# Decay rows of one head pair issued from ScalarE's queue in an attention and mixer kernel

## The chip, the cores and the metric

The kernel runs on one core of a Trainium2 chip. The metric is the device time of one execution in microseconds (us), lower is better. Of the core's engines, TensorE (PE) multiplies matrices, VectorE (DVE) and ScalarE (ACT) work element by element, GpSimd (POOL) does masks and issues most of the loads, and SyncE (SP) issues transfers. Each engine takes its instructions strictly in the order in which they stand in its own queue. A transfer (DMA) is issued by an instruction on one of these queues and tells that it has landed by a semaphore.

## The reference, cut to what matters

Eight batches of eight heads go through causal attention with a decay from a running sum, and the result goes through a mixer. The part that the change touches is the decay bias:

```python
s_pos = np.maximum(s, 0.0)
cum = np.cumsum(s_pos, axis=-1)
bias = -(cum[:, :, :, None] - cum[:, :, None, :])
scores = np.where(causal, -1000000000.0, scores + np.minimum(bias, 0.0))
```

Then follow the softmax, the product with `v`, the low-rank mixing over the sequence (`x + (xT @ U @ V)T`) and a two-layer channel mix with a residual (512 to 2048 to 512).

## The kernel before, in words

Heads are worked on in pairs: pair `n` is heads `2n` and `2n+1`, and batch 0 is the pairs 0 to 3. Each of these pairs has a buffer, a slot: partitions 0 to 63 hold the transposed `q` and `k` of both heads, and partitions 64 to 67 hold four decay rows. With them one matrix product over 68 partitions gives scores and decay bias together. The decay rows are not computed in a slot: DVE and ACT compute them for all 64 heads at once into a tile `rows` (it lies in the buffer that the profile calls `hT`; lines 221 to 228), and small transfers of 9 KB, four rows of 2304 bytes for one head, bring them to the slots (line 231). There are eight of these for batch 0, all on SP's queue, two for each pair, in the order of the pairs. After them SP stores the rows of the later batches in memory (`rows_hbm`, line 238), from where later slots are filled (line 299).

The start of the kernel, up to some 35 us, is written out by hand as a list of `step` calls (lines 1011 to 1082). The queues of DVE, ACT and SP are fixed to the order in which the program issues (`in_program_order`, line 1083). So the place of a call in the list is the place of its instructions on every engine. The pieces of the list that matter here are:

- `T0` to `T3`: the transposes of a pair on PE (line 315) into PSUM banks, and their copies into the slot (line 338). `copies` (line 289) decides who copies: of pairs 0 and 1 ACT copies the first head and DVE the second; of pair 2 ACT copies the first of four pieces and DVE the other three; of pair 3 DVE copies all four.
- `A` and `B_`: most of the scores of pair 0, which do not wait for the slot's decay rows but take them from `rows` (`near_by_rows`, line 364). Each ends with an exponential on ACT (line 395).
- `S0` to `S3`: the scores from the slots (line 402), with exponentials on ACT (lines 417, 428 and 434). A weight load of line 402 waits for the decay rows of its head.
- `spin`: products on a constant tile, whose result is not used (line 216).

PSUM has two pools here: four banks `pwork`, taken in turn, and two double banks `pscore`, taken in turn. A piece that takes a bank waits until the work on what it held before is done. POOL applies the causal masks for these four pairs (line 150), and issues loads in between.

Completion semaphores for the transfers of SP and ACT are eight counters, which the framework gives out in turn. A transfer that gets a counter for the second time waits at its issue until the counter's earlier transfer has landed. In the kernel before, the eighth row transfer waits in this way for the load of `s`, and the two stores to `rows_hbm` for the two row transfers of pair 0.

From about 35 us on, a list of words and loops interleaves the attention of later batches with the mixer of earlier ones, up to the end.

Of the kernel before, what the change touches and what calls it, by code (L numbers as in the profile page):

```python
# [39 lines left out]
def kernel(  # L40
# [12 lines left out]
    nc = tc.nc  # L53
# [11 lines left out]
    PB = NP // B  # L65
# [160 lines left out]
    nc.vector.tensor_sub(rest, cum, rows[:, 0, 1, :])  # L226
    nc.vector.tensor_copy(rows[:, 1, 1, :], rest)
    nc.vector.tensor_sub(rows[:, 2, 1, :], rest, rows[:, 1, 1, :])
    for n in range(PB):
        for hh in range(2):  # L230
            nc.sync.dma_start(
                out=slots[n][D:KA, hh, 0 : 2 * S],
                in_=rows[2 * n + hh : 2 * n + hh + 1].rearrange("n r c s -> n r (c s)"),
            )

    rows_hbm = nc.dram_tensor("rows_hbm", (4, BH, S), BF16, kind="Internal").ap()
    for r, n_r, c in ((0, 3, 1), (3, 1, 0)):
# [766 lines left out]
    def step(*gens):  # L1004
        for gen in gens:
            next(gen, None)

    def spin_some(n, ps=None):
        spin(n, (ps or pscore)()[:, 0:512])
# [7 lines left out]
    step(T0)  # L1017
    spin_some(2)
    step(T0, T0)
    step(A, A, A, A)  # L1020
    step(T1, T1, T1)
    step(B_)
# [210 lines left out]
```

The softmax here doesn't subtract the row's maximum and nothing guards it: scores larger than these inputs give would overflow.

## Time and profile before

| | |
|---|---|
| median of 13 runs | 364.79 us |
| lowest and highest of these | 364.05 and 366.83 us |
| the profiled execution's own time | 364.79 us |
| its span in the profile | 363.1 us |
| PE busy | 353.4 us (97% of the span) |
| DVE busy | 278.4 us (77%) |
| ACT busy | 209.5 us (58%) |
| POOL busy | 84.6 us (23%) |
| data moved | 37.41 MB, mean 103 GB/s |

A row of the timeline gives the start, the time from start to end of a group of like instructions, the engine (SPq is SP's queue), the source line, the operation, what it writes and reads, how often, and in brackets for how long the engine sat idle before it and what ended the wait. Instructions of one engine overlap a little in these rows: an exponential that is listed with 1.02 us is followed by the next after about 0.92 us.

### The profile page before, as it was taken

The page shows a single profiled execution, that of the slowest core. Times are in us where ns is not written, and L with a number is a line of the kernel's source. Part 1 is how long each engine was busy: PE and PEld are TensorE (multiplying, and loading weights), DVE is VectorE, ACT ScalarE, POOL GpSimd, SP SyncE. Part 2 cuts the span into 40 slices and gives each one's busy share as a digit, 9 for nine tenths or more (in the row PEclk, how much of TensorE's full clock was granted, in tenths as well). Part 3 has the DMA queues.
Part 4 walks back from the last instruction along what each step waited for, and adds up shares of the span by engine and source line. Part 5 has one row for each costly group of instructions (what it writes and reads, how often), then busy time and mean ns, then how long its engine had stood idle before and what let it go on. Part 6 is the DMA issues. An engine that isn't in the chain of part 4 may idle for free. (4 is left out here: it accounts for less than half of the span.)

```text
span 363.1 us, 9627 instructions
## 1 busy us (share of the span) xinstructions
PE 353.4 (97%) x4031; PEld 255.2 (70%) x4031; DVE 278.4 (77%) x607; ACT 209.5 (58%) x319; POOL 84.6 (23%) x108
## 2 busy tenths in 40 slices
PE   8999999999999999999999999999999999999995
PEld 3675566666588667876689667876688568678884
DVE  8875776779789758985699559975899279676976
ACT  3874975747762678247843686357834641565710
POOL 8997444314040403040314012000000000000000
PEclk9999999999999999999999999999999999999999
DMA  7999999999989998989994999271013401500063
GB/s 106 172 197 204 168 178 107 157 140 139 115 51 107 130 141 59 97 99 118 127 107 62 143 135 86 50 151 37 18 49 91 94 18 32 147 0 31 29 117 116
DMA packets 153027, 37.41 MB, mean 103 GB/s; under 512 B 136600, under 2 KB 151352, under 8 KB 152984
## 3 DMA queue, kind: packets, MB, share of 16 engines
q0 software_dynamic: 110016, 18.50, 82.9%
q1 hardware_dynamic: 42680, 18.11, 29.1%
q8 instruction: 31, 0.51, 0.6%
q10 hardware_dynamic: 288, 0.20, 0.2%
q14 instruction: 12, 0.10, 0.1%
HBM read 37.25 MB, written 9.70 MB: 129 GB/s over the span
## 5 line engine op out<-in xcount | busy, mean ns | idle before, releaser
L648 PE MATMUL pwork<-uT,w_sb 128*128 128x512 bf16 x464 | 116.6, 379 | 0.7 <-ACT hT L929 0.5
L417 ACT ACTIVATE pT<-pscore 128x1024 bf16<-128x1024 f32 x56 | 57.2, 1030 | 55.1 <-PE pscore L402 54.1
L929 ACT ACTIVATE hT<-pwork 128x512 bf16<-128x512 f32 x108 | 65.2, 609 | 31.2 <-PE pwork L648 31.1
L648 PEld LDWEIGHTS <-w_sb 128*128 128x128 bf16 x480 | 41.2, 98 | 37.3 <-issue 0.7
L402 PE MATMUL pscore<-slot 68*128 68x320 bf16 (+1 forms) x500 | 56.0, 246 | 0.2
L402 PEld LDWEIGHTS <-slot 68*128 68x128 bf16 x564 | 41.2, 97 | 16.8 <-issue 1.3
L693 PEld LDWEIGHTS <-hT 128*128 128x128 bf16 x496 | 46.1, 98 | 7.2 <-issue 0.7
L186 POOL DMA_DIRECT2D v_slot<-in_v_dram x36 | 30.3, 854 | 81.6 <-PE pwork L462 71.1
L693 PE MATMUL pwork<-w_sb,hT 128*128 128x256 bf16 x384 | 48.2, 273 | 0.0
L347 DVE TENSOR_TENSOR pT<-pT,keep 128x512 bf16<-128x512 bf16 (+1 forms) x81 | 28.7, 354 | 21.0 <-ACT pT L417 14.8
L335 DVE COPY slot<-pwork 64x576 bf16<-64x576 bf16 x76 | 34.4, 453 | 4.7 <-PE pwork L315 3.9
L462 PEld LDWEIGHTS <-pT 128*128 128x128 bf16 x870 | 32.4, 98 | 5.3 <-issue 0.6
L462 PE MATMUL pwork<-v_slot,pT 128*128 128x65 bf16 x870 | 35.5, 194 | 0.2 <-DVE uT L516 0.2
L693 PE MATMUL pwork<-w_sum,slot 128*128 128x256 bf16 x256 | 32.0, 273 | 0.8 <-DVE o_sb L707 0.7
L472 DVE TENSOR_TENSOR x_sb<-pwork,rec 128x320 bf16<-128x320 f32 x64 | 31.2, 489 | 1.3
L428 ACT ACTIVATE pT<-pscore 128x1024 bf16<-128x1024 f32 x29 | 30.2, 1042 | 2.6 <-PE pscore L402 2.4
L471 DVE RECIPROCAL rec<-pwork 128x5 f32<-128x5 f32 x64 | 12.2, 191 | 20.7 <-PE pwork L462 20.3
L693 PEld LDWEIGHTS <-slot 128*128 128x128 bf16 x256 | 24.0, 98 | 4.6 <-issue 1.6
L338 DVE COPY slot<-pwork 64x576 bf16<-64x576 bf16 x29 | 23.2, 801 | 5.1 <-PE pwork L315 3.3
L112 POOL DMA_DIRECT2D q_sd<-in_q_dram x6 | 12.6, 2105 | 44.9 <-PE pwork L315 41.3
L707 DVE TENSOR_TENSOR o_sb<-o_sb,pwork 128x512 f32<-128x512 f32 (+2 forms) x34 | 22.0, 651 | 0.7 <-PE pwork L693 0.3
L315 PEld LDWEIGHTS <-q_sd 72*128 72x128 bf16 x256 | 14.9, 97 | 8.7 <-DMA q_sd<-in_q_dram 0.9
(161 smaller groups left out, 502.1 us busy)
## 6 DMA issues: line engine op xcount, KB each, us to landing
out_dram<-o_sb SPq DMA_DIRECT2D x35, 256.0 KB
w_sb<-in_moe_w_ch_dram POOLq DMA_DIRECT2D x4, 1024.0 KB, 12.4
v_slot<-in_v_dram POOLq DMA_DIRECT2D x28, 128.0 KB, 7.1
q_sd<-in_q_dram POOLq DMA_DIRECT2D x5, 576.0 KB, 13.8
k_sd<-in_k_dram POOLq DMA_DIRECT2D x5, 576.0 KB, 17.1
q_sd<-in_q_dram POOLq DMA_DIRECT2D x4, 288.0 KB, 12.4
k_sd<-in_k_dram POOLq DMA_DIRECT2D x4, 288.0 KB, 11.4
q_sd<-in_q_dram POOLq DMA_DIRECT2D x4, 144.0 KB, 4.7
```

The costliest lines, as they stand in the source:

```text
L186: nc.gpsimd.dma_start(out=vt[:rows_t, t, :, 0:D], in_=v[b, :, ds(t * 128, rows_t), :].rearrange("h p d -> p h d"),)
L335: copies(n, hh, par)(by_run[:, :, :, par, :], src)
L338: copies(n, hh, par)(in_turn[:, :, :, :, par], src.rearrange("p c t m -> p c m t"))
L347: nc.vector.tensor_tensor(dst, dst, keep[:, :, 0:w].to_broadcast([128, n_tiles, w]), op=ALU.min)
L402: nc.tensor.matmul(dst, lhsT=slot[0:KA, hh, ds(S + j * 128, 128)], rhs=slot[0:KA, hh, lo:hi], start=True, stop=True,)
L417: nc.scalar.activation(pT[:, hh, 0:1024], near, EXP, scale=scale)
L428: nc.scalar.activation(pT[:, :, 1024:1536], mid.rearrange("p (a b) -> p a b", a=2), EXP, scale=scale)
L462: nc.tensor.matmul(po[:, i, :], lhsT=pT[:, hh, ds(place(j, i), 128)], rhs=vt[:, j, h, :], start=(j == 0), stop=(j == i), skip_group_check= ...
L472: nc.vector.tensor_tensor(x_sb[:, hp, :, ds(hh * D, D)], po[:, :, 0:D], rec.to_broadcast([128, 5, D]), op=ALU.mult,)
L648: nc.tensor.matmul(f1, lhsT=w1_sb[:, kt, ds(nf * 128, 128)], rhs=u[:, kt, :], start=(kt == 0), stop=(kt == 3),)
L693: nc.tensor.matmul(acc[:, i, :], lhsT=a[:, kt, ds(i * 128, 128)], rhs=b[:, kt, :], start=(i == 0 and kt == 0), stop=(kt == HF - 1), skip_g ...
L929: nc.scalar.activation(hT[:, nf, :], f1, RELU)
```

## The change

The row transfers of pairs 0, 2 and 3 stay on SP's queue, in that order. The two of pair 1 are issued from ACT's queue, behind the third step of `T0` and ahead of `A`.

```diff
-    for n in range(PB):
+
+    def rows_to_slot(n, queue):
         for hh in range(2):
-            nc.sync.dma_start(
+            queue.dma_start(
                 out=slots[n][D:KA, hh, 0 : 2 * S],
                 in_=rows[2 * n + hh : 2 * n + hh + 1].rearrange("n r c s -> n r (c s)"),
             )
+
+    for n in (0, 2, 3):
+        rows_to_slot(n, nc.sync)
...
     step(T0)
     spin_some(2)
     step(T0, T0)
+    rows_to_slot(1, nc.scalar)
     step(A, A, A, A)
     step(T1, T1, T1)
     step(B_)
```

The built program then has these waits on ACT's queue (line 232 is the transfer, 342 the copy that was line 338, 399 the exponential that was line 395):

```
L342 copy slot0 x2            waits for PE
L232 transfer slot1, head 0   waits for DVE and ACT (the rows are computed)
L232 transfer slot1, head 1   waits for completion counter 1
L399 exponential of A         waits for PE
L342 copy slot1 x2            waits for PE
L342 copy slot2               waits for PE
L399 exponential of B_        waits for PE
```

Completion counter 1 belongs to the first row transfer of pair 0, on SP's queue. Compute instructions stand in the same order as before on every engine.

## The prediction

> **What bounds the kernel now.** I read the page first, for the engine that is never idle, then the waits, for how long it is, and then the timeline of the first 20 us, engine by engine, since the change lies there.
>
> ```profile
> PE 353.4 (97%) x4031; PEld 255.2 (70%) x4031; DVE 278.4 (77%) x607; ACT 209.5 (58%) x319; POOL 84.6 (23%) x108
> PE   8999999999999999999999999999999999999995
> ACT  3874975747762678247843686357834641565710
> PEclk9999999999999999999999999999999999999999
> DMA  7999999999989998989994999271013401500063
> ```
>
> The reader is to see that PE is full from the second slice of nine us to the last but one, while ACT is not. There is no slack behind the opening in which lost time could be won back: in the waits of PE after 24 us the longest sum is 0.9 us, and none of them is for a transfer. So what the opening loses should be lost at the end. In the opening itself PE is not alone in the bound. This is ACT's part of the timeline:
>
> ```profile
> 6.45 1.61 ACT L338 COPY slot<-pwork 64x576 bf16<-64x576 bf16 x2 [0.47 <-PE pwork L315]
> 9.26 1.02 ACT L395 ACTIVATE pT<-pscore 128x1024 bf16<-128x1024 f32 x1 [1.20 <-PE pscore L364]
> 10.18 1.60 ACT L338 COPY slot<-pwork 64x576 bf16<-64x576 bf16 x2
> 12.03 0.80 ACT L338 COPY slot<-pwork 64x576 bf16<-64x576 bf16 x1 [0.25 <-PE pwork L315]
> 13.16 1.02 ACT L395 ACTIVATE pT<-pscore 128x1024 bf16<-128x1024 f32 x1 [0.33 <-PE pscore L364]
> 14.08 1.02 ACT L428 ACTIVATE pT<-pscore 128x1024 bf16<-128x1024 f32 x1
> ```
>
> Between 8.06 us and 9.26 us ACT has nothing to do, and from there to 15 us it has gaps of 0.25 and 0.33 us alone. The hole of 1.20 us is where the change puts two transfers. Now who waits for ACT (DVE), and what PE does (PE):
>
> ```profile
> 12.86 5.76 DVE L338 COPY slot<-pwork 64x576 bf16<-64x576 bf16 x7 [1.34 <-ACT slot L338]
> ...
> 15.38 0.59 PE L216 MATMUL pwork<-busy 128*128 128x512 bf16 x2 [0.26 <-DVE slot L338]
> 15.81 0.61 PE L402 MATMUL pscore<-slot 68*128 68x128 bf16 x6
> 16.25 0.81 PE L216 MATMUL pwork<-busy 128*128 128x512 bf16 x3
> ```
>
> This is a chain: ACT's copy of pair 2 (12.03 to 12.83) lets DVE begin at 12.86 with its three copies for pair 2, and the third ends at about 15.3 (12.86 + 3 x 0.82), when a PSUM bank comes free for PE's spin at 15.38, behind which the scores of pair 1 stand at 15.81. The transfers in question, on SP:
>
> ```profile
> 8.20 5.10 SPq L231 DMA_DIRECT2D slot<-hT  x8
> 13.34 0.92 SPq L238 DMA_DIRECT2D rows_hbm<-hT  x2
> ```
>
> Eight issues, the first of 0.76 us and the later ones 0.57, one each 0.615 us. The landing records in the trace say when all increments of each had come: pair 0 at 12.1 and 12.3 us, pair 1 at 13.8 and 15.76, pair 2 at 16.0 and 16.4. Pair 1's second one is what a weight load of line 402 waits for:
>
> ```profile
> PEld L402 <- DMA slot<-hT: 0.3, 1, 0.3
> ```
>
> That wait ends at 15.80, when the spins of 15.38 (two of 0.21 us each) are through as well.
>
> **The change part by part.**
>
> SP loses two issues, 1.23 us. Pairs 2 and 3 and the stores to `rows_hbm` are issued that much sooner. Nobody waits for them before (no row of the waits names them), so this is worth nothing; the cover is that pair 2's rows, at 16.0 us, are first used at 17.5.
>
> ACT gains two issues. The rows are ready at 8.11 us (DVE line 228), ACT is free at 8.06, so the first goes out at 8.15. A row for an issue on ACT stands at the end of the trace (line 785, two in 0.86 us, 0.43 each); SP's same transfer takes 0.57. I take 0.57; both ends, 0.43 and 0.76, are in the range. Were this all, ACT would be back at about 9.3 us, and the exponential of `A` would be late by nothing or 0.1 us.
>
> But the second issue adds a wait. It gets completion counter 1, and waits for the first row transfer of pair 0, which SP issues at 8.20. That landed at 12.1 us before. It is still SP's first, so it should land then again, give or take 0.3 us for the ACT transfer beside it, which brings 9 KB to the same engines. A rule speaks of this time. The row: issue at 8.20, its first packets at 10.60, landed at 12.1, so 2.4 us to the first packet and 3.9 in all, with the DMA row of the page at 9. The Trainium skill, "DMA: Bandwidth & Descriptors", section "Latency and other measured facts", puts the first byte of a transfer from these queues at about 0.6 us. By the rule the landing would be at 8.20 + 0.6 + 1.5 = 10.3 us, by the trace at 12.1. I take the trace, where the same transfer is measured under the same load.
>
> Behind that wait on ACT's in-order queue stand the exponential of `A`, two copies of pair 1, one of pair 2, and the exponential of `B_`. Followed through:
> - second issue 12.15 to 12.72; exponential of `A` at 12.72 in place of 9.26, late by 3.46;
> - copies of pair 1 from 12.72 + 0.92 = 13.64 to 15.2 (PE had the inputs by 10 us);
> - copy of pair 2 at 15.25 in place of 12.03, late by 3.2: the gap of 0.25 ahead of it is eaten;
> - exponential of `B_` at 16.0 in place of 13.16, late by 2.85.
>
> DVE starts its pair 2 copies at 16.08 in place of 12.86. The third ends at 18.55, so PE's spin goes at 18.6 in place of 15.38, late by 3.2. PE meanwhile stops first for the PSUM of `A` (S0 at 13.7 in place of 13.05), then for the bank that ACT's pair 1 copies hold (15.2), then for pair 2's banks (16.9). All of it is done by 18.6. Scores of pair 1, head 1, then come at 19.0.
>
> The rows of pair 1: the first lands at about 12.2 and is used at 17.2. The second is issued at 12.15; transfers issued between 10.3 and 12.7 took 4.2 to 5.5 us to land, so 16.4 to 17.7, ahead of 19.0. So the 0.33 us wait goes and is worth nothing, as the spins end with it. If the landing took 7 us, it would be next late.
>
> From 18.6 on PE, ACT and DVE have the same work in the same order. PE was busy 4.69 of 5 us between 15 and 20 us and 4.90 of the next 5, so at most some 0.4 us is to be made up; I take 0.2. POOL is late by less: its masks start at 15.52 because of its own issues before, and the load issued at 16.93 goes at about 18.4, but its users are late by 3.2. At 28 us PE stood 0.9 us for nothing the profile shows; it could shrink or grow, plus or minus 0.9.
>
> Sum: 0 (SP) + 3.2 (wait and issue, through DVE's chain) - 0.2 = +3.0 us. The profiled execution's own time, 364.79 us (span 363.1 and 1.7 around it), is the median itself. So 364.8 + 3.0 = **367.8 us**.
>
> A second rule weighs on the gaps. The row: the first nine spins took 3.62 us, 0.40 each, and those at 15.38 take 0.21, so this PE starts at half speed, although the PEclk row says 9 throughout. The Trainium skill, "TensorE: Matmul & The Clock Gate", "Part 1: The HAM clock gate", says the half clock returns after one idle window of about 3.4 us. In the changed kernel PE works some 1.9 us of the 5.5 between 13.05 and 18.6, in pieces no more than 1.1 us apart. No window is idle, so by its wording nothing is lost; if a thin window counts as idle, one window at half speed costs up to 3.4 / 2 = 1.7 us. I leave it at 0, and 1.7 goes to a rival.
>
> **The rivals.**
>
> 1. *The wait is short.* The landing comes as the rule has it, at 10.3. Then the second issue ends at 10.9, `A` at 10.9, pair 2's copy at 10.9 + 0.92 + 1.62 = 13.45, late by 1.4. Time: 366.2. For it: the DMA load might fall differently with another queue in use. Against: the measured 3.9 us.
>
> 2. *The clock falls.* The delay of 3.0 and 1.7 more for half-speed products, 369.5. For it: the opening is padded with spins on a constant tile, so it is meant to be kept busy, and the gaps triple. Against: the longest gap is a third of a window.
>
> 3. *Not slower: the wait is no wait, and ACT's hole covers both issues.* The point from which it decides is the landing of counter 1: before about 9.0 us, ACT is at work by 9.5 and the 0.25 and 0.33 us gaps swallow the rest. Then rows of pair 1 land at about 12.3, the 0.33 us wait on them goes, and the best is 364.8 - 0.33 = 364.5. Against: it needs 0.8 us from issue to landing, where the quickest in the trace, the load of `s`, took from 0.82 to 3.43. That the waits on the counter are not as built is the same case. A late landing that PE makes up later belongs here too, in time: 364.5 to 365.3.
>
> **How the numbers follow.** What a measurement of this kernel can tell from no change is about 0.2%, 0.73 us. Forecast 0.70, its own range 366.6 to 368.9 (landing 0.3 either way, issue -0.15 to +0.2, gap of 28 us, made up 0 to 0.4); rival 1 0.12; rival 2 0.10; rival 3 0.08, of which 0.03 faster by over 0.2% and 0.05 within. All else is slower: 0.92. The range takes in the forecast and rival 1 and stops where rival 2 begins to: 366.1 to 369.4.
>
> **What would show it.** In ACT's timeline: the two issues, with some 3.4 us between the start of the first and of the second, and `A`'s exponential at 12.7 us with no wait for PE; the copy of pair 2 at 15.25. In DVE's: the seven copies at 16.1, with an idle time of 4 us or more ahead of them for ACT. In PE's: the spin before pair 1's second head at 18.6, late by 3.2, and every later row late by about 3. Wrong if `A`'s exponential is at about 9.3, if a row transfer of pair 1 is waited for, or if rows after 40 us are late by less than 1.

## The result, and the profile after

| | us |
|---|---|
| before, median of 48 runs | 364.66 |
| changed, median of 11 runs | 371.26 (lowest 368.40) |
| ratio to before, with its 95% interval | 1.0152 (1.0132 to 1.0173) |
| changed, taken again beside the experiments, median of 6 | 371.40; ratio 1.0181 (1.0127 to 1.0234) |

The change makes the kernel slower by some 6.6 us by the medians. The ratio compares means and leaves out executions more than 1.5% above the fastest of their kernel (of the changed one those of 609.67 and 374.35 us), and by it the loss is some 5.5 us. The direction was forecast, the size was not: 367.8 us in a range of 366.1 to 369.4. The execution that was profiled first took 609.67 us, with PE's clock near half from beginning to end, and none of the others came near it; so all rows below are from a second profile of the same kernel, of an execution of 371.8 us (span 370.1).

The clock that counts here is the granted clock, the share of full speed that the profile shows PE to have been given. The page of that second profile has in its clock row what before had not:

```profile
PEclk9759999999999999999999999999999999999999
```

A digit is a slice of 9.25 us: the second and the third, 9 to 28 us, hold a stretch at half speed. The trace's clock records give it exactly: half from 13.82 to 27.48 us, four times 3.41 us. Busy time by stage from the same profile (start and end, length, then busy us and number of instructions of PE, weight loads, DVE, ACT and POOL, then the granted clock, DMA share and GB/s):

```profile
8.00:12.00 4.00, 4.00 (x59) 2.84 (x57) 3.28 (x5) 0.70 (x1) 3.53 (x9) 1.00 1.13 160
12.00:16.00 4.00, 2.39 (x26) 1.65 (x25) 0.00 (x0) 2.02 (x3) 4.00 (x7) 0.73 1.19 161
16.00:20.00 4.00, 3.01 (x27) 2.20 (x27) 2.59 (x4) 3.27 (x6) 1.56 (x4) 0.50 1.29 186
20.00:24.00 4.00, 4.00 (x20) 2.21 (x19) 3.03 (x4) 2.13 (x3) 2.77 (x7) 0.50 1.07 181
24.00:28.00 4.00, 4.00 (x31) 1.81 (x30) 0.00 (x0) 3.02 (x4) 2.74 (x5) 0.57 0.75 121
```

ACT does 0.70 us of work between 8 and 12 us, and PE is thin (busy for part of the time only) from 12 to 20. From 20 us on PE is full again, but of 20 products in 4 us, which is the half clock. Now ACT's timeline, the hole and what is in it:

```profile
7.08 1.62 ACT L342 COPY slot<-pwork 64x576 bf16<-64x576 bf16 x2 [0.98 <-PE pwork L319]
8.25 5.68 ACTq L232 DMA_DIRECT2D slot<-hT  x2
13.97 1.02 ACT L399 ACTIVATE pT<-pscore 128x1024 bf16<-128x1024 f32 x1 [5.27 <-PE pscore L368]
14.89 2.41 ACT L342 COPY slot<-pwork 64x576 bf16<-64x576 bf16 x3
17.17 1.01 ACT L399 ACTIVATE pT<-pscore 128x1024 bf16<-128x1024 f32 x1
```

The two issues span 5.68 us. In the trace the first took 1.16 us (8.25 to 9.41) and the second 0.59 (13.33 to 13.92); between them ACT waited for completion counter 1, whose last increment came at 13.31. The row of 13.97 puts its idle time down to PE; but PE's last products for `A` were done at 9.54 (a row of line 368, 8.94 and 0.60 long), and what released ACT is the landing. In between ACT did none of the work that stands behind the issue in its queue. This is what a wait for a transfer looks like when the engine's next compute row carries it. DVE and PE behind it:

```profile
17.33 5.76 DVE L342 COPY slot<-pwork 64x576 bf16<-64x576 bf16 x7 [5.51 <-ACT slot L342]
```

```profile
15.04 1.01 PE L406 MATMUL pscore<-slot 68*128 68x320 bf16 x4 [1.61 <-ACT pT L399]
16.53 0.27 PE L406 MATMUL pwork<-slot 68*128 68x64 bf16 x2 [0.47 <-ACT slot L342]
...
19.84 1.01 PE L216 MATMUL pwork<-busy 128*128 128x512 bf16 x2
20.65 1.06 PE L406 MATMUL pscore<-slot 68*128 68x128 bf16 x6
```

The chain is the forecast's: DVE's copies at 17.33 in place of 12.86 (late by 4.47), PE's spin at 19.84 in place of 15.38 (4.46). The two spins then take 0.81 us to the next row, where they took 0.43.

**The account.** Later rows of the two profiles: the exponential of pair 3's first head 29.47 in place of 21.69, late by 7.78; the transposes of the first `mix_first` piece (before's line 603) 33.97 in place of 26.18, 7.79; those of the next piece, behind the stop at 28 us, 35.88 in place of 28.92, 6.96; the end 370.1 in place of 363.1, 7.0. So 4.46 us come from ACT's wait, 3.32 are added up to 29.5 us while the clock is half, 0.83 are won back at the stop at 28 us (before, PE stood 0.88 us there), and nothing changes after that. The rows of the two pieces, first before, then changed:

```profile
26.18 0.39 PE L603 MATMUL pwork<-identity,x_sb 128*128 128x128 bf16 x4
28.89 0.19 PE L462 MATMUL pwork<-v_slot,hT 128*128 128x65 bf16 x1 [0.88 <-issue]
28.92 0.39 PE L603 MATMUL pwork<-identity,x_sb 128*128 128x128 bf16 x4
...
33.97 0.39 PE L607 MATMUL pwork<-identity,x_sb 128*128 128x128 bf16 x4
35.88 0.39 PE L607 MATMUL pwork<-identity,x_sb 128*128 128x128 bf16 x4
```

Of the 13.65 us at half clock, the first 6 cost nothing: until 19.84 PE waits for ACT and DVE in any case, and their rows above (13.97 to 17.33 us) are not held up by products at half speed. The remaining 7.64 us, up to 27.48, would cost half of that, 3.82 us, if PE did nothing but products at half speed; it cost 3.32.

### The profile page after: what moved, and what is told of

Same layout as the page of the kernel before. It is cut to its first block, busy times and chain, and to the rows that moved or that the text cites. A ratio compares the mean times of both kernels' runs of the same rounds, so it can differ in the third digit from the quotient of the medians.

```text
span 608.0 us, 9627 instructions
## 1 busy us (share of the span) xinstructions
PE 602.7 (99%) x4031; PEld 364.2 (60%) x4031; DVE 288.0 (47%) x607; ACT 222.2 (37%) x319; POOL 85.2 (14%) x108
## 4 chain that ended last, share of the span: by engine, by line
PE 99%; ACT 0%; DVE 0%; issue 0%
PE pwork L652 30%; PE pwork L697 28%; PE pscore L406 12%; PE pwork L466 8%; PE pwork L319 5%; PE parts L857 5%; PE pwork L662 4%; PE pscore L368 1%; PE pscore L652 1%; PE pscore L216 1%; PE pwork L857 1%; PE pwork L216 1%; PE pwork L495 1%; PE pwork L406 1%; PE pwork L781 1%; PE pscore L540 0%
## 5 line engine op out<-in xcount | busy, mean ns | idle before, releaser
L652 PE MATMUL pwork<-uT,w_sb 128*128 128x512 bf16 x464 | 198.2, 576 | 0.1
L652 PEld LDWEIGHTS <-w_sb 128*128 128x128 bf16 x480 | 52.2, 120 | 80.8 <-issue 76.9
L406 PE MATMUL pscore<-slot 68*128 68x320 bf16 (+1 forms) x500 | 89.4, 343 | 0.0
L406 PEld LDWEIGHTS <-slot 68*128 68x128 bf16 x564 | 64.0, 137 | 35.3 <-issue 28.4
L697 PE MATMUL pwork<-w_sb,hT 128*128 128x256 bf16 x384 | 80.5, 386 | 0.0
L697 PEld LDWEIGHTS <-hT 128*128 128x128 bf16 x496 | 61.9, 129 | 29.8 <-issue 3.5
L466 PEld LDWEIGHTS <-pT 128*128 128x128 bf16 x870 | 50.9, 119 | 10.7 <-issue 9.1
L466 PE MATMUL pwork<-v_slot,pT 128*128 128x65 bf16 x870 | 53.2, 231 | 0.0
L697 PE MATMUL pwork<-w_sum,slot 128*128 128x256 bf16 x256 | 53.2, 388 | 0.0
L697 PE MATMUL pwork<-w_sb,v_slot 128*128 128x256 bf16 x128 | 27.4, 387 | 0.0
```

Source lines behind the costliest of these rows:

```text
L406: nc.tensor.matmul(dst, lhsT=slot[0:KA, hh, ds(S + j * 128, 128)], rhs=slot[0:KA, hh, lo:hi], start=True, stop=True,)
L466: nc.tensor.matmul(po[:, i, :], lhsT=pT[:, hh, ds(place(j, i), 128)], rhs=vt[:, j, h, :], start=(j == 0), stop=(j == i), skip_group_check= ...
L652: nc.tensor.matmul(f1, lhsT=w1_sb[:, kt, ds(nf * 128, 128)], rhs=u[:, kt, :], start=(kt == 0), stop=(kt == 3),)
L697: nc.tensor.matmul(acc[:, i, :], lhsT=a[:, kt, ds(i * 128, 128)], rhs=b[:, kt, :], start=(i == 0 and kt == 0), stop=(kt == HF - 1), skip_g ...
```

## The experiments

| kernel | median us (runs) | ratio to before (95%) | start of `A`'s exponential | mean granted clock by execution |
|---|---|---|---|---|
| changed, again | 371.40 (6) | 1.0181 (1.0127 to 1.0234) | 13.97 | 0.968 to 0.990 |
| head 0 alone on ACT | 364.59 (14) | 0.9996 (0.9970 to 1.0022) | 9.57 | 0.997 to 1.000, one 0.985 |
| nine copies on ACT, no transfer moved | 370.50 (6) | 1.0143 (1.0105 to 1.0182) | 13.97 | 0.985 to 0.990 |
| five copies on ACT | 370.47 (4) | 1.0122 (1.0044 to 1.0201) | 11.20 | 0.980 to 0.999 |
| two copies on ACT | 365.36 (12) | 1.0016 (0.9981 to 1.0052) | 9.56 | 0.996 to 1.000, two 0.985 and 0.987 |
| both transfers on ACT, stores from GpSimd | 365.16 (14) | 1.0007 (0.9985 to 1.0029) | 10.16 | 0.996 to 1.000 |
| changed, with spins in PE's gaps | 369.47 (6) | 1.0124 (1.0074 to 1.0174) | 13.24 | 0.990 to 1.000 |
| before, without its spins behind 13 us | 367.78 (13) | 1.0079 (1.0054 to 1.0105) | 9.45 | 0.969 to 0.986 |

### The changed kernel again

No edit.

> The changed kernel once more, for a profile at its usual time (about 371 us). Theory W+C (the wait on completion counter 1 holds ACT, and the thin PE work in that hole makes the PE clock fall back to half for several windows): the exponential of A at about 12.7 to 13.9 us, the PE rows after it at 0.40 us per 512 columns for some 7 to 15 us, mean granted clock 0.98 to 0.99, and 3 to 6 us of the time lost in that stretch. Theory W alone (the wait and nothing else): all PE rows after 6 us at 0.21 us per 512 columns, and a time of about 368 us.

It came out as the first theory had it, the wait and the clock; the rows are those above. All six executions had a clock below 1 (0.968 to 0.990), where 15 of 19 of the kernel before beside them had 0.997 or more. The wait alone was expected to give about 368. Over the executions of the changed kernel in both measurements, apart from that of 609.67 us, the time goes with the clock: the six at 0.990 or 0.991 took 369.3 us on average, the eight at 0.980 to 0.985 took 371.2, and the three at 0.968 to 0.972 took 374.1.

### Only the first head on ACT

```diff
-    for n in (0, 2, 3):
-        rows_to_slot(n, nc.sync)
+    for n, heads in ((0, (0, 1)), (1, (1,)), (2, (0, 1)), (3, (0, 1))):
+        rows_to_slot(n, nc.sync, heads)
...
-    rows_to_slot(1, nc.scalar)
+    rows_to_slot(1, nc.scalar, (0,))
```

> Only pair 1's first head goes on ACT's queue, which needs no wait on a counter; its second head stays on SP's in its old place. Theory W+C: ACT is back at about 9.4 us, A's exponential is at 9.3 to 9.5, clock 1.00 and the time of the kernel before, 364.7, give or take 0.5. Rival I (the issue on ACT itself, or a second queue beside SP's, costs the time): half or more of the loss stays, 367 to 369 us.

364.59, the time of before. ACT's timeline:

```profile
8.34 1.18 ACTq L232 DMA_DIRECT2D slot<-hT  x1
9.57 1.02 ACT L399 ACTIVATE pT<-pscore 128x1024 bf16<-128x1024 f32 x1 [1.55 <-PE pscore L368]
```

One issue of 1.18 us fits into the hole, and a second queue by itself costs nothing that this measurement can tell. The loss comes with the second issue. The profiled execution happened to be the one of fourteen in which the clock fell (369.18 us), half from 11.57 to 21.81 us. `A`'s exponential was at 9.57 all the same, so the clock can fall without ACT being late; see the kernel without spins.

### ACT held by other work

```diff
     step(T0, T0)
+    for _ in range(9):
+        nc.scalar.copy(pTs[1][:, 0, 0:512], busy)
     step(A, A, A, A)
```

> The kernel before with its transfers untouched, and nine ACT copies of a constant tile (about 0.5 us each, some 4.5 us in all) in the place where the change puts its two issues; they are work that the kernel does not need. Theory W+C: it is the time for which ACT is held that counts, not the transfers, so A's exponential is at about 12.7, the clock falls as in the changed kernel, and the time is 369 to 372. Rival T (the order in which the rows land, or two queues on the same DMA engines, costs the time): the loss is no more than what ACT lost, 3 us, with the clock at 1.00, about 367.5.

```profile
8.13 5.82 ACT L1021 COPY pT<-busy 128x512 bf16<-128x512 bf16 x9
13.97 1.02 ACT L395 ACTIVATE pT<-pscore 128x1024 bf16<-128x1024 f32 x1
```

The copies took 0.65 us each, not 0.5, and so ACT is held until 13.97, to the hundredth as in the changed kernel. The time is 370.50, against 371.40, and the clock falls in every execution. No transfer was moved here. So ACT's lateness is enough for the loss, and it brings the clock's fall with it; whose rows land when, or on whose queue, need not come into it. The 0.9 us between the two kernels lies within the intervals of their ratios.

The same with five copies:

> The same with five ACT copies, some 2.5 us, of which 1.2 us lie in ACT's hole, so that A's exponential is late by about 1.4 us. Theory W+C: a window of thin PE work is not reached or only in some executions, so the time is that of ACT's delay alone, about 366, clock 0.995 or more. If the loss is in proportion to the delay, with no threshold, it is 366 to 367 with the clock at 0.99.

`A`'s exponential came at 11.20, late by 1.94. The four executions do not agree: 366.39 with a clock of 0.999, which is about the delay alone, and 369.78, 371.41 and 371.15 with 0.994, 0.980 and 0.980. So a smaller hold can have nearly the full price or about a quarter of it. In the profiled one of 369.78 us the clock stayed up past the hold; PE then stood 2.45 us for nothing that the profile shows, at the product where before it stood 0.88 us, and the clock was at half behind that stop, from 32.21 to 35.62 us. Its 5.0 us of span over before are thus 1.7 of ACT's delay (that product's row starts at 28.62 in place of 26.91), 1.6 of the longer stop and, as the rest, 1.7 with the half clock. Neither the stop nor the clock behind it was expected; with four runs, two of them at a low clock and not profiled, the price of a smaller hold stays open.

And with two:

> The kernel before with two ACT copies in the place of the change's issues, 1.3 us by what the nine took (0.65 us each), so A's exponential is at about 9.4 instead of 9.26. Theory W+C: inside ACT's hole, so no change, 364.3 to 365.2 us, clock 1.00. If any work in the hole costs its own time, 366.

365.36, slightly above what was expected, and within its interval of no change. `A`'s exponential is 0.30 us late, and `B_`'s at 13.17 in place of 13.16: the hole takes two copies. Two of twelve executions had a low clock, where a clock of 1.00 was expected; in the kernel before beside them it was six of 36 (0.986 or less).

### Both transfers on ACT, without the wait

```diff
     for r, n_r, c in ((0, 3, 1), (3, 1, 0)):
-        nc.sync.dma_start(
+        nc.gpsimd.dma_start(
             out=rows_hbm[ds(r, n_r), ds(2 * PB, BH - 2 * PB)].rearrange("r n s -> n r s"),
```

The two stores leave the eight counters, so that ACT's second transfer gets the counter of the load of `s`.

> The changed kernel with both row transfers of pair 1 on ACT as it has them, but the two stores to the row buffer in memory issued from GpSimd. With two transfers fewer on the completion counters ahead of it, ACT's second transfer gets the counter of the load of s, which landed long before. Theory W+C: the wait is all, so ACT is back at about 10 us, A's exponential at about 10.0 instead of 14.0, and the time is 364.7 to 365.5 with the clock at 1.00 in most executions. Rival I (two issues on ACT cost the time): 368 to 371 us.

```profile
8.30 1.81 ACTq L232 DMA_DIRECT2D slot<-hT  x2
10.16 1.02 ACT L399 ACTIVATE pT<-pscore 128x1024 bf16<-128x1024 f32 x1 [1.92 <-PE pwork L319]
11.08 2.43 ACT L342 COPY slot<-pwork 64x576 bf16<-64x576 bf16 x3
13.38 1.01 ACT L399 ACTIVATE pT<-pscore 128x1024 bf16<-128x1024 f32 x1
```

Two issues back to back take 1.81 us and not 5.68, `B_`'s exponential is late by 0.22, and the time is 365.16. With the wait gone the change is worth nothing, as its two transfers were forecast to be. This is the experiment that puts the loss on the counter.

### Spins in PE's gaps

```diff
                 if (n, hh) == (3, 0):
-                    spin(2, tile)
+                    spin(6, tile)
...
+    spin(8, raw[1, 1])
     step(S0, S0)
+    spin(6, raw[1, 1])
...
         yield
+        if n == 0:
+            spin(5, raw[1, 1])
         for hh in range(2):
             mm(tail[:, ds(hh * 64, 64)], hh, 4, 512, S)
```

Here `raw[1, 1]` is the PSUM bank of pair 1's second head, which DVE has emptied by then.

> The changed kernel with 23 more products on the constant tile in PE's gaps while ACT is held (8 ahead of S0, 5 between its two parts, 6 behind it, 4 more in T3). They keep a PSUM bank longer, so pair 3's transposes wait for DVE's third copy: by the durations of the changed kernel's second profile the scores of pair 1, head 1, are then late by about 5.3 us against the kernel before. Theory W+C: the clock stays at 1.00 in most executions, so only that delay is left, less up to 0.8 at the 28 us stop: 369.3 to 370.1 us, below the changed kernel although PE does 4.9 us of work more. Rival (the loss is not the clock's, only waits): the spins change nothing or add to it, 371 to 373 us.

369.47, with 4.9 us of work more on PE. The six executions are of two kinds: 368.44, 368.68 and 368.78 with a clock of 0.999 or 1.000, and 370.16, 371.81 and 371.98 with 0.994 and 0.990. So the clock held in half of them, not in most as expected. The profiled one is of the first kind:

```profile
12.00:16.00 4.00, 3.95 (x35) 2.24 (x33) 0.00 (x0) 2.73 (x4) 4.00 (x7) 1.00 1.27 170
16.00:20.00 4.00, 4.00 (x38) 2.27 (x37) 2.75 (x4) 2.53 (x4) 2.34 (x5) 1.00 1.27 181
```

```profile
20.48 0.61 PE L408 MATMUL pscore<-slot 68*128 68x128 bf16 x6
```

Pair 1's second head comes at 20.48, late by 4.67, nearly as in the changed kernel, and yet this execution ends 3.4 us sooner (span 366.7 against 370.1). With PE kept busy the clock stays, in half of the executions, and what is left is ACT's delay: the span is 3.6 us over that of before, close to what the account has without the clock (4.46 less 0.83). Between the three at full clock (368.6 on average) and the two with 0.990 (371.9) lie 3.3 us. That is about the 3.32 us of the account, but from few executions, and the slower ones were not profiled.

### Without spins

```diff
-    S0, S1, S2, S3 = (scores(n, pT_of(n), {1: (2, 3), 3: (2, 0)}.get(n, ())) for n in range(PB))
+    S0, S1, S2, S3 = (scores(n, pT_of(n), ()) for n in range(PB))
...
-                if (n, hh) == (3, 0):
-                    spin(2, tile)
...
-        spin(2, pvs[0])
```

> The kernel before without the eleven products on the constant tile behind 13 us (two ahead of T3, five in S1, two in S3, two ahead of the values' tiles); transfers as before. They are 2.3 us of PE work. Theory C (thin PE windows of 3.4 us let the clock fall, whatever makes them thin): the clock falls in part of the executions at least, 0.98 to 0.99, and the time is 365 to 370. Rival (the clock needs a wait of several us to fall): clock 1.00, and 363 to 364.7 us.

All thirteen executions lost the clock (0.969 to 0.986), and the time went up by 3 us although PE had 2.3 us less to do. The edit only takes work away.

```profile
8.00:12.00 4.00, 3.66 (x51) 2.48 (x50) 3.37 (x5) 2.68 (x4) 3.53 (x8) 0.95 1.09 141
12.00:16.00 4.00, 4.00 (x31) 2.61 (x30) 2.04 (x4) 1.61 (x2) 4.00 (x8) 0.50 1.33 166
```

In the profiled execution, the slowest of the thirteen, the clock fell at 11.57, ahead of the place of the first spin taken away. That one fall cannot be laid on the edit, as the kernels are alike up to there; it looks like the fall that the kernel before, with its spins, shows in six of 36 executions. The edit shows in that the clock is low in all thirteen.

## Why the prediction was wrong

- *Which issues move, and what SP gains.* Right. SP's six issues took 3.94 us, the stores were issued from 12.2 on, and nobody gained by it: with the wait gone, the time is that of before. One reading under it was too broad. The waits of before do name the stores: SP's first fill of a later slot (line 299) waited 3.2 us for them. No compute engine did, so the term of nothing stands.
- *ACT's second issue waits for counter 1.* Right, and it is the cause of ACT's delay.
- *When counter 1 is complete.* The term of 12.1 us, "give or take 0.3 us for the ACT transfer beside it", was too small: 13.31. In four profiles without a transfer on ACT it was 11.63 to 12.05 beside the 12.11 of before, in four with one 12.20 to 13.31. That is 0.1 to 1.2 us later. These are single executions, so that the transfer on ACT delays the one on SP is likely and not shown. It moved `A`'s exponential from the forecast 12.72 to 13.97, and DVE's start from 16.08 to 17.33: 1.25 us. The rule that was weighed there, which put the landing at 10.3, was further off. With this miss alone the time would have been about 364.8 + 4.46 - 0.83 = 368.4 us, inside the range.
- *The chain from ACT through DVE to PE's spin.* Right in every link, with that 1.25 added: 4.46 where 3.2 was forecast.
- *The clock, costed at nothing.* This step failed, and was the larger miss. "No window is idle, so by its wording nothing is lost" read the rule of the Trainium skill, "TensorE: Matmul & The Clock Gate", "Part 1: The HAM clock gate", word for word. The forecast looked for a loss in the thin stretch from 13.05 to 18.6 us and found no idle window in it; the clock fell at 13.82 us, and in the 3.41 us up to there PE's rows are idle for the last 0.4 alone. So the rule as worded does not cover these runs: a window need not be idle. With the spins taken out and no wait added, the clock was low in all thirteen executions. The rival had the effect but not its size: one window, 1.7 us. It was four windows, of which the part behind ACT's wait cost nothing and the last 7.64 us cost 3.3.
- *Made up.* 0.2 was forecast, with 0.9 either way for the stop at 28 us; it was 0.8, of that stop.

Together: 3.0 forecast, plus 1.25 for the landing, plus 3.3 for the clock, less 0.6 more made up, 7.0, which is the span's growth.

What stays open is which window lets the clock fall. The clock records change in steps of 3.41 us that begin at another time in each execution. Here are five such windows, the first two with a fall at their end (changed kernel; head 0 alone), the other three without one (before; five copies; two copies). The first number behind the length is PE's busy time:

```profile
10.41:13.82 3.41, 3.03 (x43) 2.11 (x42) 1.40 (x2) 0.00 (x0) 3.06 (x8) 1.00 1.21 168
8.16:11.57 3.41, 3.25 (x47) 2.27 (x48) 2.94 (x5) 1.99 (x3) 2.94 (x8) 1.00 1.14 159
7.78:11.20 3.42, 3.26 (x48) 2.19 (x47) 3.14 (x5) 2.21 (x4) 2.95 (x8) 1.00 1.12 163
15.14:18.56 3.42, 2.46 (x29) 1.64 (x29) 3.33 (x5) 2.78 (x5) 3.42 (x7) 1.00 1.48 206
26.74:30.16 3.42, 1.76 (x40) 1.60 (x40) 1.73 (x8) 0.58 (x1) 3.04 (x7) 1.00 1.13 208
```

A window of 3.25 us of busy time came before a fall, and one of 1.76 did not. So the busy time of PE's rows in one window does not decide, and the runs give no threshold. What they show is how often: with ACT held as long as in the change, or with the spins gone, every execution had a clock of 0.991 or less, and the kernel before had one in six of 36.

## What to carry to other kernels

A transfer's issue can hold the engine that issues it for longer than an issue takes, here 5.68 us in place of 1.81: look up which completion counter it gets and whose landing it must wait for, because everything behind it on that queue waits too. In an opening padded to hold PE's clock, cost each new gap of PE twice, once for the delay and once for the clock, and look at the granted clock of several executions before trusting one. To see which part is which, hold the engine for as long with other work, and fill PE's gap with work that is not needed.

## What the runs showed of the hardware that was not expected

- The first row transfer on ACT took 1.16 to 1.18 us to issue in four profiles, where SP's first takes 0.76; the second took 0.59.
- The clock fell after a window in which PE was idle for 0.4 of 3.41 us, and came back one to six windows later (3.4 us in the kernel with five copies, 6.8 with nine, 10.2 with head 0 alone, 13.65 in the changed one, 20.5 in the one without spins). In the last of these PE's rows were busy for 19.9 of the 20.5 us.
- At one product near 28 us PE stood for nothing that the profile shows: 0.88 us before, hardly at all in the changed kernel, 1.61 us in the one with two copies, 2.45 us in the one with five. A stop like this can move a measured delay by some 2 us; its cause stays open.
